# Group 0 of a fused attention and Fourier mixing kernel: plain products on resident weights, with the weights' combinations made for the later groups only

## The chip, the cores and the metric

One core of a Trainium2 chip. The metric is the device time of one execution in microseconds (us), the median of the executions named. Engines: PE is TensorE's matmuls, DVE VectorE, ACT ScalarE, POOL GpSimd, SP SyncE, which issues every large transfer of this kernel in one queue.

## The reference, cut to what matters

```python
# q, k, v: (8, 8, 576, 64) fp32; moe_w_ch1: (512, 2048), moe_w_ch2: (2048, 512)
x  = attention with softmax over the head dimension of q and over the sequence of k    # (8, 576, 512)
u  = x + real(fft(fft(x, axis=1), axis=2))
un = (u - mean) / sqrt(var + 1e-6)
return u + relu(un @ w_ch1) @ w_ch2
```

The kernel works in nine groups of 512 tokens. Each batch has a *front* (attention, Fourier transforms, normalisation); the front of batch g+1 is issued beside the two layers of group g.

## The kernel before

The two weight matrices arrive as 64-bit words that must be *converted* to fp32: 32 blocks of 128 x 512. From group 0 on both layers of the kernel before use Strassen's seven products of half blocks, so the weights are also *combined*: from four quarters, three more are made by adding and subtracting. Converted and combined weights are stored to scratch memory, from which every later group reloads them.

```python
def prepare(self, layer, p, places):
    w = self.wtile()                                        # one of 4 buffers
    for i in range(2):
        self.convert(places[i], w[:, 2 * i:2 * i + 2, :]...)        # ACT, DVE, POOL
    (self.b_side if layer else self.a_side)(lambda i: w[:, i, :], nc.gpsimd, nc.vector)
    if layer == 0:
        nc.sync.dma_start(self.w1s[p][:], w[:, 0:7, :])
        self.stream[p] = w                                  # used where it lies
    else:
        nc.sync.dma_start(self.w2s[:, :, p, :]..., w[:, 0:7, :])    # all 7 parts of pair p

def load(self, n):                                          # one reload: layer 2 takes ONE part of ALL 8 pairs
    ...
        self.nc.sync.dma_start(w[:], self.w2s[B_AT[ORDER[i - NP]]])

# group 0, in program order (start): products of layer 1 between the preparations
steps += [ready(0, 0), fetch_in(0, 3, 0)] + [ready(0, p) for p in range(1, 4)]
steps += jobs[0] + [ready(0, 4), ready(0, 5)] + jobs[1] + [ready(0, 6), ready(0, 7), fetch_in(1, 0, 12)]
steps += jobs[2] + [ready(1, 0), fetch_out(1, False), ready(1, 1)] + jobs[3]
for p in range(2, NP):
    steps += [fetch_out(p, p % 2 == 0), ready(1, p)]
return steps + [lambda i=i: blk.load(NP + i) for i in range(4)]
```

A tile framework orders the instructions of each engine and sets the semaphores; within an engine they run in that order.

Of the kernel before, what the change touches and what calls it, by code (L numbers as in the profile page):

```python
# [41 lines left out]
P = 128  # L43
# [13 lines left out]

A_AT = {1: 0, 2: 1, 3: 6, 4: 3, 5: 4, 6: 5, 7: 2}
B_AT = {1: 0, 2: 2, 3: 3, 4: 6, 5: 4, 6: 5, 7: 1}
ORDER = (1, 6, 5, 7, 2, 4, 3)  # L60
# [3 lines left out]

def merged(main, side):

    done = 0
    for i, step in enumerate(main):
        step()
        upto = (i + 1) * len(side) // len(main)  # L70
        while done < upto:
            side[done]()
            done += 1
    for step in side[done:]:
        step()
# [24 lines left out]
class _Block:  # L100
    def __init__(self, ctx, tc, q, kT, v, w1, w2, ft, cd, out):
# [27 lines left out]
        for t in (self.ZT, self.Zx, self.ZTr):  # L129
# [5 lines left out]
                      for p in range(2)]  # L135
        self.ft = c.tile([P, 7, NM], F32, name="ft")
# [27 lines left out]
    def wtile(self):  # L164
        return self.work.tile([P, NP, HD], F32, tag="w", name="w", bufs=4)

    def words(self, layer, f, place):

        if layer == 0:
            w1 = self.w1.bitcast(I32).rearrange("(k p) n -> p k n", p=P)  # L170
            self.nc.sync.dma_start(place.bitcast(I32).rearrange("p (k n) -> p k n", k=KT),
                                   w1[:, :, f * 2 * P:(f + 1) * 2 * P])
        else:
            w2 = self.w2.bitcast(I32).rearrange("(f p) n -> p f n", p=P)
            self.nc.sync.dma_start(place.bitcast(I32), w2[:, f, :])

    def convert(self, place, t):
        nc, V = self.nc, self.nc.vector
        pair = place.bitcast(I32).rearrange("p (n w) -> p n w", w=2)
        lo, hi = pair[:, :, 0], pair[:, :, 1]  # L180
        ti = t.bitcast(I32)

        nc.scalar.activation(lo, lo.bitcast(U32), ACT.Copy, scale=2.0 ** -29)

        V.tensor_scalar(out=ti, in0=hi, scalar1=3, scalar2=0x3FFFFFFF, op0=ALU.logical_shift_left,
                        op1=ALU.bitwise_and)
        V.scalar_tensor_tensor(out=ti, in0=hi, scalar=-(1 << 30), in1=ti, op0=ALU.bitwise_and, op1=ALU.bitwise_or)

        least = float(np.array(0x38100000, np.uint32).view(np.float32))
        nc.scalar.activation(hi.bitcast(F32), hi.bitcast(F32), ACT.Abs)  # L190
        V.scalar_tensor_tensor(out=t, in0=hi.bitcast(F32), scalar=least, in1=t, op0=ALU.is_ge, op1=ALU.mult)
        nc.gpsimd.tensor_tensor(out=ti, in0=ti, in1=lo, op=ALU.add)  # L192

    def a_side(self, at, e1, e2):

        e1.tensor_tensor(out=at(4), in0=at(2), in1=at(3), op=ALU.add)  # L196
        e1.tensor_tensor(out=at(2), in0=at(0), in1=at(2), op=ALU.subtract)
        e2.tensor_tensor(out=at(5), in0=at(4), in1=at(0), op=ALU.subtract)
        e2.tensor_tensor(out=at(6), in0=at(1), in1=at(5), op=ALU.subtract)

    def b_side(self, at, e1, e2):

        e1.tensor_tensor(out=at(4), in0=at(1), in1=at(0), op=ALU.subtract)
        e2.tensor_tensor(out=at(1), in0=at(3), in1=at(1), op=ALU.subtract)
        e1.tensor_tensor(out=at(5), in0=at(3), in1=at(4), op=ALU.subtract)
        e1.tensor_tensor(out=at(6), in0=at(2), in1=at(5), op=ALU.subtract)

    def prepare(self, layer, p, places):

        nc = self.nc  # L210
        w = self.wtile()
        for i in range(2):
            self.convert(places[i], w[:, 2 * i:2 * i + 2, :].rearrange("p a n -> p (a n)"))
        (self.b_side if layer else self.a_side)(lambda i: w[:, i, :], nc.gpsimd, nc.vector)
        if layer == 0:
            nc.sync.dma_start(self.w1s[p][:], w[:, 0:7, :])
            self.stream[p] = w
        else:
            nc.sync.dma_start(self.w2s[:, :, p, :].rearrange("s p n -> p s n"), w[:, 0:7, :])

    def load(self, n):

        g, i = divmod(n, NP + 7)
        if g > B:
            return
        w = self.wtile()
        if i < NP:
            self.nc.sync.dma_start(w[:, 0:7, :], self.w1s[i][:])
        else:
            self.nc.sync.dma_start(w[:], self.w2s[B_AT[ORDER[i - NP]]])  # L230
        self.stream[n] = w

# [227 lines left out]
    def norm(self, g):  # L460
# [31 lines left out]
        def all_stats():  # L492
# [4 lines left out]
        return unT, [all_stats] + pipelined(range(4), [normal, turn]) + [  # L497
            lambda: self.b_side(lambda i: unT[:, i], V, nc.gpsimd)]
# [7 lines left out]


# [35 lines left out]
    def up(self, g, unT, h):  # L543
# [3 lines left out]
        for j in range(NP // 2):  # L547
            pairs = (2 * j, 2 * j + 1)
            at = lambda i, j=j: h[:, 2 * j:2 * j + 2, i, :]

            def product(m, bank, first, last, pairs=pairs):
                def run(i):
                    w = self.stream[15 * g + pairs[i]]
                    for k in range(2):
                        nc.tensor.matmul(bank()[:, i, :], lhsT=w[:, A_AT[m], k * P:(k + 1) * P],  # L555
                                         rhs=unT[:, B_AT[m], k, :], start=first and i == 0 and k == 0,
                                         stop=k == 1,
                                         skip_group_check=True)
                return [lambda i=i: run(i) for i in range(2)]
# [4 lines left out]
            def other(i, at=at):  # L564
                def run(bank, u):
                    V.tensor_tensor(out=at(i), in0=bank[:], in1=u[:], op=ALU.add)  # L566
                    nc.scalar.activation(at(i), at(i), ACT.Relu)  # L567
                    if i == 2:
                        self.a_side(at, nc.gpsimd, nc.gpsimd)
                return run  # L570
# [5 lines left out]
    def used(self, n):  # L576
        self.stream.pop(n)
        if n >= NP:
            self.load(n + 4)

    def down(self, g, h):
        nc, V = self.nc, self.nc.vector

        def product(m, bank, first, last):
            n = 15 * g + NP + ORDER.index(m)

            def run(i, q):
                w = self.stream[n]
                for p in range(4 * q, 4 * q + 4):
                    nc.tensor.matmul(bank()[:, i, :], lhsT=h[:, p, A_AT[m], i * P:(i + 1) * P], rhs=w[:, p, :],  # L590
# [48 lines left out]
def kernel(ctx: ExitStack, tc: tile.TileContext, q, kT, v, w1, w2, ft,  # L639
# [34 lines left out]
    hpool = ctx.enter_context(tc.tile_pool(name="h", bufs=1))  # L674

# [3 lines left out]
    for step in front(0):  # L679
        step()  # L680
    for step in norm(0):
        step()
    for g in range(B + 1):
        unT = nexts.pop(g)
        h = hpool.tile([P, NP, 7, HD], F32, tag="h", name="h")
        jobs, down = blk.up(g, unT, h), blk.down(g, h)
        if g + 1 < B:
            side = front(g + 1)
        else:
            side = blk.reload() if g + 1 == B else []  # L690
        cut = len(side) * 2 // 3
        if g == 0:
            first = start(blk, jobs, h)
            merged(first, side[:cut])
        else:

            merged(flat(jobs), side[:cut])
        merged(down, side[cut:] + (norm(g + 1) if g < B else []))


def start(blk, jobs, h):


    at = h[:].rearrange("p a s n -> p (a s n)")
    inside = lambda r: at[:, r * 2 * D:(r + 1) * 2 * D]
    places = {}

    def fetch(layer, p, where):
        places[layer, p] = where
        for i in range(2):  # L710
            blk.words(layer, p + i * NP, where[i])

    def prepare(layer, p):
        blk.prepare(layer, p, places.pop((layer, p)))

    def fetch_in(layer, p, r):
        return lambda: fetch(layer, p, [inside(r), inside(r + 1)])

    def fetch_out(p, spare):
        def run():  # L720
            if spare:
                t = blk.work.tile([P, 7, 2, HD], F32, tag="unT", name="words", bufs=1)[:].rearrange(
                    "p a k n -> p (a k n)")
            else:
                t = blk.wtile()[:].rearrange("p a n -> p (a n)")
            fetch(1, p, [t[:, i * 2 * D:(i + 1) * 2 * D] for i in range(2)])
        return run

    def ready(layer, p):
        return lambda: prepare(layer, p)  # L730

    steps = [fetch_in(0, p, 2 * p) for p in range(3)] + [fetch_in(0, p, 2 * p - 2) for p in range(4, NP)]
    steps += [ready(0, 0), fetch_in(0, 3, 0)] + [ready(0, p) for p in range(1, 4)]
    steps += jobs[0] + [ready(0, 4), ready(0, 5)] + jobs[1] + [ready(0, 6), ready(0, 7), fetch_in(1, 0, 12)]
    steps += jobs[2] + [ready(1, 0), fetch_out(1, False), ready(1, 1)] + jobs[3]
    for p in range(2, NP):
        steps += [fetch_out(p, p % 2 == 0), ready(1, p)]
    return steps + [lambda i=i: blk.load(NP + i) for i in range(4)]
# [48 lines left out]
```

## Time and profile before

| | kernel before |
|---|---|
| time, median of 3 | 1392.67 us (1391.23 to 1393.92) |
| profiled span, mean granted clock of PE | 1384.5 us, 0.919 |
| group 0's first layer starts / its second layer / group 1 / group 2 | 110.25 / 289.8 / 338.2 / 464.5 us |

The prediction below shows the stages and the costliest waits. Two lines of the page give the whole: busy time of each engine, and PE's granted clock in 40 slices of 34.6 us, in tenths.

```profile
PE 1226.2 (89%) x5676; PEld 1003.1 (72%) x5676; DVE 580.0 (42%) x1146; ACT 326.7 (24%) x590; POOL 422.1 (30%) x350
...
PEclk7558785589999999999999999999999999999996
```

PE is busy 89% of the span, but the clock is 5 to 8 tenths in the first nine slices, that is up to 311 us. What releases PE between 110 and 290 us, in sum (us in all, times, longest):

```profile
engine line waited for: us in total, times, longest us
PE tr L486 <- DVE eo L479: 24.4, 2, 23.3
PE bb L555 <- DVE u L525: 23.9, 3, 8.7
```

And SP's queue late in that stretch. L219 stores one pair's combined quarters of W2, L230 reloads one part of all eight pairs:

```profile
257.44 0.38 SPq L219 DMA_DIRECT2D w2s<-w  x1
...
264.55 0.38 SPq L219 DMA_DIRECT2D w2s<-w  x1
...
275.77 0.38 SPq L219 DMA_DIRECT2D w2s<-w  x1
...
280.52 16.75 SPq L230 DMA_DIRECT2D w<-w2s  x5
```

The stores come as the preparations are done, here 7 to 11 us apart; the last is issued at 275.77, the reloads from 280.52 on, and only at 289.8 does the second layer start. Its first product needs a part from every pair, so by the code no product of the layer can start before the last pair is made, stored and reloaded. The trace alone doesn't show this wait: PE has no idle time just ahead of 289.8. After the 23.3 us of idle it turns batch 1's normalised tokens (from 260.3) and then works off the beginning of batch 2's front, which the framework put there.

### The profile page before, as it was taken

To read this page: it belongs to the slowest core of one execution; us is meant where nothing else is said; L and a number is where in the kernel's file an instruction comes from. 1 tells how busy PE (TensorE), PEld (TensorE's weight loads), DVE (VectorE), ACT (ScalarE), POOL (GpSimd) and SP (SyncE) were. 2 spreads that over 40 slices of the span, in tenths; PEclk is the share of its full clock that TensorE was granted. 3 is DMA by queue.
4 is the path that set the end of the run, shared out by engine and by line. 5 is a ranking of instruction groups with operands and counts; after the bars stand their busy time and mean duration, and the time that the engine had idled before them with its cause. 6 is when DMAs were issued, how large, how long until landed. Compare 5 with 4: busy or idle time off the path is not lost.

```text
span 1384.5 us, 14661 instructions
## 1 busy us (share of the span) xinstructions
PE 1226.2 (89%) x5676; PEld 1003.1 (72%) x5676; DVE 580.0 (42%) x1146; ACT 326.7 (24%) x590; POOL 422.1 (30%) x350
## 2 busy tenths in 40 slices
PE   4578677399899998999999999999999999999992
PEld 3437563288787876788778877887788778788882
DVE  3948876821513254335713542364234242502200
ACT  2624342410310142114301421142014101201200
POOL 1624566710530125003600450045013401321310
PEclk7558785589999999999999999999999999999996
DMA  5922334575342543156424542454253335455421
GB/s 170 306 68 69 137 128 163 190 265 164 141 152 88 172 159 146 67 167 198 158 98 138 193 159 77 145 197 152 88 146 130 150 103 174 150 178 179 165 102 45
DMA packets 90279, 203.46 MB, mean 147 GB/s; under 512 B 22241, under 2 KB 56033, under 8 KB 82145
## 3 DMA queue, kind: packets, MB, share of 16 engines
q1 hardware_dynamic: 90208, 202.52, 43.2%
q8 instruction: 45, 0.74, 0.2%
q14 instruction: 26, 0.20, 0.0%
HBM read 177.33 MB, written 29.88 MB: 150 GB/s over the span
## 4 chain that ended last, share of the span: by engine, by line
PE 74%; DVE 10%; POOL 6%; DMA 4%; issue 2%; ACT 1%; SPq 0%; POOLq 0%; DVEq 0%; ACTq 0%
PE bb L590 14%; PE bb L555 11%; PE bc L590 9%; PE ba L590 9%; PE ba L555 7%; PE bc L555 6%; PE acc L402 5%; DMA q<-in_q_dram 3%; PE acc L289 3%; PE acc L427 2%; POOL w L192 1%; PE acc L424 1%; PE tr L486 1%; PE acc L405 1%; POOL eo L384 1%
## 5 line engine op out<-in xcount | busy, mean ns | idle before, releaser
L555 PE MATMUL bb<-unT,w 128*128 128x256 f32 x864 | 218.8, 395 | 46.6 <-DVE u L525 39.6
L555 PEld LDWEIGHTS bb<-unT,w 128*128 128x128 f32 x864 | 166.5, 197 | 78.3 <-DVE u L525 46.3
L590 PE MATMUL bb<-w,h 128*128 128x256 f32 x864 | 198.5, 381 | 0.0
L590 PEld LDWEIGHTS bb<-w,h 128*128 128x128 f32 x864 | 161.5, 190 | 28.4 <-issue 7.3
L555 PE MATMUL ba<-unT,w 128*128 128x256 f32 x576 | 142.5, 387 | 0.0
L196 POOL TENSOR_TENSOR h<-h 128x512 f32<-128x512 f32 x36 | 46.1, 1279 | 313.4 <-ACT h L567 313.4
L555 PE MATMUL bc<-unT,w 128*128 128x256 f32 x576 | 140.5, 381 | 0.0
L590 PE MATMUL bc<-w,h 128*128 128x256 f32 x576 | 131.4, 381 | 0.0
L590 PE MATMUL ba<-w,h 128*128 128x256 f32 x576 | 128.0, 379 | 0.0
L590 PEld LDWEIGHTS bc<-w,h 128*128 128x128 f32 x576 | 107.5, 190 | 18.0 <-issue 4.4
L555 PEld LDWEIGHTS ba<-unT,w 128*128 128x128 f32 x576 | 109.2, 194 | 15.7 <-issue 1.0
L590 PEld LDWEIGHTS ba<-w,h 128*128 128x128 f32 x576 | 109.2, 190 | 15.4 <-issue 0.8
L555 PEld LDWEIGHTS bc<-unT,w 128*128 128x128 f32 x576 | 107.0, 190 | 15.3 <-DVE h L566 0.9
L567 ACT ACTIVATE h<-h 128x512 f32<-128x512 f32 x108 | 68.1, 631 | 190.8 <-DVE h L566 190.5
L604 POOL TENSOR_TENSOR x<-x,u 128x512 f32<-128x512 f32 x18 | 23.3, 1293 | 254.4 <-DVE u L528 172.2
L402 PE MATMUL acc<-ft,eo 128*128 128x289 f32 (+3 forms) x240 | 83.3, 472 | 7.5 <-POOL eo L386 7.4
L402 PEld LDWEIGHTS acc<-ft,eo 128*128 128x128 f32 (+3 forms) x240 | 39.6, 183 | 42.3 <-issue 26.0
L525 DVE TENSOR_TENSOR u<-bb,s 128x512 f32<-128x512 f32 x45 | 31.0, 689 | 89.1 <-PE bb L555 54.3
L318 POOL TENSOR_TENSOR q<-q,qm 128x512 f32<-128x512 f32 x36 | 41.8, 1170 | 82.2 <-DVE qm L317 33.1
L528 DVE TENSOR_TENSOR u<-bb,s 128x512 f32<-128x512 f32 x45 | 31.0, 689 | 77.5 <-PE bb L555 45.4
L289 PE MATMUL acc<-v,ks 128*128 128x128 f32 (+1 forms) x320 | 55.5, 317 | 6.1 <-ACT ks L277 4.1
L566 DVE TENSOR_TENSOR h<-bc,u 128x512 f32<-128x512 f32 x72 | 49.6, 689 | 24.0 <-PE bc L555 23.0
(134 smaller groups left out, 1540.0 us busy)
## 6 DMA issues: line engine op xcount, KB each, us to landing
w<-w2s SPq DMA_DIRECT2D x63, 1024.0 KB
w<-w1s SPq DMA_DIRECT2D x64, 896.0 KB
k<-in_kT_dram SPq DMA_DIRECT2D x32, 288.0 KB
h<-in_w_dram SPq DMA_DIRECT2D x18, 512.0 KB
v<-in_v_dram SPq DMA_DIRECT2D x32, 256.0 KB
q<-in_q_dram SPq DMA_DIRECT2D x32, 256.0 KB
w1s<-w SPq DMA_DIRECT2D x8, 896.0 KB
w2s<-w SPq DMA_DIRECT2D x8, 896.0 KB
```

Source lines behind the costliest of these rows:

```text
L196: e1.tensor_tensor(out=at(4), in0=at(2), in1=at(3), op=ALU.add)
L289: nc.tensor.matmul(pk, lhsT=ks[0:n, c, :], rhs=v[0:n, c, :], start=(c == 0), stop=(c == NC - 1))
L318: nc.gpsimd.tensor_tensor(out=heads, in0=heads, in1=spread(m), op=ALU.subtract)
L402: nc.tensor.matmul(pz, lhsT=eo[c][int(odds)][s, cols], rhs=self.ft[s, 3 * int(odds) + c, :], start=(c == 0), stop=(c == 2 and odds))
L427: nc.tensor.matmul(pb, lhsT=z(2 + k), rhs=self.cd[:, 2 + k, 0:HD - 1], start=(k == 0), stop=(k == 1))
L525: V.tensor_tensor(out=temp("u2"), in0=box["bb"][:], in1=box["s1"][:], op=ALU.add)
L528: V.tensor_tensor(out=temp("u3"), in0=box["bb"][:], in1=box["s1"][:], op=ALU.add)
L555: nc.tensor.matmul(bank()[:, i, :], lhsT=w[:, A_AT[m], k * P:(k + 1) * P], rhs=unT[:, B_AT[m], k, :], start=first and i == 0 and k == 0, s ...
L566: V.tensor_tensor(out=at(i), in0=bank[:], in1=u[:], op=ALU.add)
L567: nc.scalar.activation(at(i), at(i), ACT.Relu)
L590: nc.tensor.matmul(bank()[:, i, :], lhsT=h[:, p, A_AT[m], i * P:(i + 1) * P], rhs=w[:, p, :], start=first and i == 0 and p == 0, stop=p == ...
L604: nc.gpsimd.tensor_tensor(out=x, in0=x, in1=t[:], op=ALU.add)
```

## The change

The intent: group 0 alone computes whole products, two layers of 16 blocks on the converted weights where they lie in SBUF, so it needs no combined weights. The combinations, needed from group 1 on, are to be made beside its second layer. One large tile holds the converted W1, W2 and group 0's hidden layer; later it holds the ring of loads and the later hidden layers. The conversion is rewritten with one two-input DVE operation in place of two.

```diff
+        self.big = c.tile([P, 3 * NF * D], F32, name="big")
+        self.w1sb, self.w2sb, self.h0 = part(0), part(1), part(2)
...
+        def fetch(i):          # words of block i; most lie in w2sb until they are converted
+            if i < NF + 12 or i == NF + 13:
+                raw = self.w2sb[:, at:at + 2, :]...
+            else:              # W2's blocks 12, 14, 15: the place of the normalised input
+                    spare[0] = self.work.tile([P, 7, 2, HD], F32, tag="unT", name="words", bufs=1)
...
+            nc.scalar.activation(t, hi.bitcast(F32), ACT.Abs)
+            V.tensor_scalar_max(t, t, least)
-            V.tensor_scalar(out=ti, in0=hi, scalar1=3, scalar2=0x3FFFFFFF, ...)
+            V.tensor_scalar(out=ti, in0=ti, scalar1=3, scalar2=0x3FFFFFFF, ...)
             V.scalar_tensor_tensor(out=ti, in0=hi, scalar=-(1 << 30), in1=ti, ...)
-            V.scalar_tensor_tensor(out=t, in0=hi.bitcast(F32), scalar=least, in1=t, op0=ALU.is_ge, op1=ALU.mult)
+            nc.scalar.activation(lo, lo.bitcast(U32), ACT.Copy, scale=2.0 ** -29)
+            nc.gpsimd.tensor_tensor(out=out.bitcast(I32), in0=ti, in1=lo, op=ALU.add)
...
+    def combine(self, layer, p):
+        for i in range(2):     # three temporaries in turn, free when their store is done
+            tag = ("s1", "u2", "u3")[(2 * (NP * layer + p) + i) % 3]
+            t.append(self.work.tile([P, 2, HD], F32, tag=tag, name=tag, bufs=1))
...
+    def plain(self, g, unT):
+        def up(f):
+            n = ("ba", "bb")[f % 2]
+            ph = self.ps.tile([P, 512], F32, tag=n, name=n)
+            for k in range(KT):
+                nc.tensor.matmul(ph[:], lhsT=self.w1sb[:, f, k * P:(k + 1) * P], rhs=unT[...], ...)
+            if f % 2:
+                nc.vector.tensor_scalar_max(h[:, f, :], ph[:], 0.0)
+            else:
+                nc.scalar.activation(h[:, f, :], ph[:], ACT.Relu)
+        def part(i, n):        # 16 products of 512 columns into one bank, "bc"
...
+            for f in range(NF):
+                convert(f)
+                if f + 8 < 2 * NF:
+                    fetch(f + 8)
+                up[f]()
+            for f in range(NF):
+                if f == 0:
+                    fetch(NF + 12)
+                    fetch(NF + 14)
+                convert(NF + f)
+                after = {4: 8, 5: 9, 6: 10, 7: 11, 11: 13, 12: 15}
+                if f in after:
+                    fetch(NF + after[f])
+            combine = [lambda l=l, p=p: blk.combine(l, p) for l in range(2) for p in range(NP)]
+            combine[NP:NP] = [lambda i=i: blk.load(15 + i) for i in range(4)]
+            side += norm(1)
+            merged(down, mixed(side, combine))
```

Cut: the new numbering of the parts, the ring of loads in the large tile, and the old `start`, which goes.

## The prediction

> **What bounds the kernel now.** I read the windows view first, cut where the PE timeline shows stages to begin: group 0's first layer (110.25), its second layer (289.8), group 1 (338.2), group 2 (464.5).
>
> ```profile
> core 0: us, PE busy (x) PEld busy (x) DVE busy (x) ACT busy (x) POOL busy (x), PEclk, DMA share, GB/s
> ...
> 70.00:110.25 40.25, 28.44 (x62) 14.70 (x63) 22.32 (x59) 12.23 (x23) 9.91 (x11) 0.52 0.24 80
> 110.25:205.00 94.75, 70.89 (x345) 60.38 (x345) 78.07 (x128) 34.31 (x63) 52.63 (x43) 0.86 0.32 107
> 205.00:289.80 84.80, 51.61 (x155) 32.98 (x154) 58.30 (x111) 29.64 (x52) 50.00 (x42) 0.54 0.62 206
> 289.80:338.20 48.40, 48.40 (x226) 42.61 (x225) 9.26 (x19) 2.72 (x5) 5.90 (x5) 1.00 0.54 182
> 338.20:464.50 126.30, 121.09 (x569) 100.16 (x568) 40.33 (x79) 24.49 (x44) 34.23 (x28) 1.00 0.39 134
> 464.50:1384.50 920.00, 872.09 (x4185) 726.48 (x4184) 327.65 (x668) 194.39 (x352) 240.09 (x189) 0.98 0.42 142
> ```
>
> From 289.8 on PE is the bound: 1042 of 1095 us busy, granted clock 0.98 to 1.00. The 179.6 us from 110.25 to 289.8 are different: PE is busy 122 us, partly at half clock, and DVE is busy 136 us, POOL 103 us. Those are the weights' words being converted and combined. The PE timeline shows where it hurts (start, length, line):
>
> ```profile
> 133.15 1.89 PE L555 MATMUL ba<-unT,w 128*128 128x256 f32 x8
> 142.63 3.78 PE L555 MATMUL bb<-unT,w 128*128 128x256 f32 x8 [7.59 <-DVE u L525]
> ...
> 234.98 2.07 PE L427 MATMUL acc<-cd,Z 128*128 128x255 f32 x4
> 260.30 1.97 PE L486 MATMUL tr<-ident,eo 128*128 128x128 f32 x8 [23.26 <-DVE eo L479]
> ...
> 289.79 7.13 PE L590 MATMUL ba<-w,h 128*128 128x256 f32 x32
> 296.76 7.07 PE L590 MATMUL bb<-w,h 128*128 128x256 f32 x32
> ```
>
> PE waits 7.6 us for an eviction that stands behind conversions in DVE's queue, and 23.3 us for the next batch's normalisation, for the same reason. After such a gap eight instructions take 3.78 us in place of 1.89. The last two rows give the steady rate: 32 instructions in 6.9 us, 0.216 us each, two instructions to a product. The groups of 110 to 290 give what one conversion costs DVE:
>
> ```profile
> L191 DVE SCALAR_TENSOR_TENSOR w<-h,w 128x512 f32<-128x512 f32 x10 | 13.8, 1392 | 0.1
> L187 DVE SCALAR_TENSOR_TENSOR w<-h,w 128x512 int32<-128x512 int32 x10 | 10.4, 1051 | 0.0
> L185 DVE TENSOR_SCALAR w<-h 128x512 int32<-128x512 int32 x10 | 7.6, 774 | 0.2 <-PE bc L555 0.2
> L192 POOL TENSOR_TENSOR w<-w,h 128x512 int32<-128x512 int32 x10 | 14.2, 1423 | 5.3 <-DVE qrec L322 2.5 <-DVE w L191 2.0 <-issue 0.7
> ```
>
> The means are stretched: in the timeline the same L187 takes 0.69 us alone and up to 1.77 us beside POOL.
>
> **What the Trainium skill says.** "SBUF — State Buffer", section Who interferes with whom: GpSimd shares a read and write port pair with DVE; a DVE operation with two SBUF inputs, or a two-port mode, and a GpSimd operation lock each other out. The 0.69 against 1.77 us agrees. "TensorE: Matmul & The Clock Gate", section What's actually happening: half clock until about 3.4 us of sustained work, and again after an idle window. The trace agrees (3.78 after a gap of 7.6 us; a gap of 3.33 us at 362 did not bring it). "VectorE: DVE Perf Modes", section The perf-mode tier table: fp32 tensor_scalar in SBUF gets 2x, two-input operations 1x. The trace agrees: unstretched 0.42 us for L185, 0.69 for L187.
>
> **The change, part by part.** The instruction order of the two kernels can be compared, since the changed one builds; no time is taken from it. From group 2 on PE's order is the same. So I estimate when group 2 starts (464.5 now) and leave the 920 us after it.
>
> (a) Front of batch 0. Now group 0 starts at 110.25 with 8 of the 32 conversions done. In the new order all 16 of layer 1 stand before it, and two combinations. A conversion is now two tensor_scalar and one two-input operation: 0.42+0.42+0.69 = 1.53 us of DVE unstretched, against 0.42+0.69+0.69 = 1.80. Eight more are 12 us of DVE and 10 us of POOL (1.27 each). Between 70 and 110 DVE has 18 us idle and POOL 30, so most of it hides; a few operations stand on the chain of normalisation. Start: 112 us (110 to 119).
>
> (b) First layer. 16 x 4 products of 512 columns, two instructions of 2 x 0.216 each: 128 x 0.43 = 55 us, against 224 x 0.216 = 48 us for the seven products per pair. But of batch 1's front nearly nothing stands between them. What can stretch it is DVE: odd blocks are evicted there (relu), each bank has one buffer, and between the relu of block 1 and of block 15 DVE's order has 9 conversions, 23 combinations of 256 columns, 7 relus and batch 1's q work. Stretched: 9 x (0.75+0.75+0.91) = 21.7; 23 x 0.69 = 15.9; 7 x 0.69 = 4.8; q work 7.3; together 50 us, for 14 blocks that PE does in 14 x 3.45 = 48. In sum it balances, but it is loaded in front: 11.5 us lie between the relus of blocks 1 and 3, and 11.8 between 3 and 5, against 6.9 of PE. So I add 9 us of waiting and 3 us of half clock at the start. First layer: 67 us, ending at 179.
>
> (c) Second layer with the whole front of batch 1 beside it: 55 us of plain products, plus the front. From the timeline at full clock a front is: four k rows of 2.0, four q of 1.35, tails 2.0, first transform 10.1, second 5.0, turns 1.8, about 32 us. Three weight blocks wait for a buffer that frees only as layer 1 ends (two fetches of 512 KB, a conversion, a third fetch, a conversion: about 18 us); PE reaches them after 14 to 20 us, so little is lost. Four results share one bank: about 1 us each where nothing fills in. I put 8 us for these and for the normalisation chain. Total 95 us, group 1 starts at 274.
>
> (d) Group 1: 448 x 0.216 = 96.7, plus the front of batch 2, 32 us, plus the usual 2.5 us of waits: 131 us (now 126.3, because a third of that front was already done at 290). Group 2 starts at 405.
>
> So 464.5 - 405 = 59 us. PE's arithmetic grows by 14 us; the gaps that go are worth 73. The stores to the scratch weights and their reload are as many bytes as before and fall in a stage with room: at most some 15 MB in 67 us, 224 GB/s, against 302 GB/s reached at 35 to 70. I shade the gain to 57: 1392.7 - 57 = 1336 us.
>
> **Rivals.** *DVE and POOL remain the bound.* The conversions and combinations are all still there, now in 70 us in place of 180. If the port pair were wholly exclusive, POOL's work up to the end of layer 1 (about 63 us) and DVE's two-input and two-port work (about 70) would need 133 us from 33 on, so layer 1 could not end before 166, and at 85% use not before 189. For it: the stretched means. Against it: in 35 to 70 now, both did more unstretched work (about 42 us) than a wholly exclusive port allows in 35. It makes 10 to 20 us less gain: 1346 to 1356. *Head of line in the DMA queue.* All transfers are issued in order from one queue, stores that wait for combinations stand before fetches, and fetches of blocks 8 to 11 wait for conversions. Then ACT and DVE stand at a conversion while relus queue behind, and PE falls to half clock: 1350 to 1360. *PE alone is the bound.* Evictions keep up, layer 1 takes 58 and the second 90: 1322. *Nothing is won,* because what is removed returns as 14 us of products and a longer group 1: that needs 45 us of new waits, which I see no place for.
>
> **Range and chances.** The sum rests mostly on known PE counts; the uncertain terms are the start (+7), layer 1 (-9 to +15) and the second layer (-5 to +8). Range 1318 to 1356. The 2% line is at 1364.8, so faster 0.93, within 2% 0.06, slower 0.01.
>
> **What would show it.** Right: layer 1 starting at 110 to 119 and taking 60 to 75 us with DVE over 80% busy, PE's waits there being for DVE relus and none above 8 us; group 1 starting near 274; granted clock near 1.0 from 125 on, where it is 0.54 to 0.86 now; an unchanged 920 us after group 2's start. Wrong if PE waits for POOL or DMA in layer 1, if the blocks fetched last stop the second layer over 5 us, if batch 1's front leaves gaps over 10 us there, or if groups 2 to 8 get longer because loads and h share one tile.

## The result and the profile after

| | before | after |
|---|---|---|
| median, us (4 runs each, side by side) | 1391.95 (1387.39 to 1393.92) | 1329.29 (1327.89 to 1332.62) |
| profiled span, us | 1384.5 | 1327.7 |
| mean granted clock of PE | 0.919 | 0.968 |
| layer 1 starts / layer 2 / group 1 / group 2, us | 110.3 / 289.8 / 338.2 / 464.5 | 113.2 / 181.9 / 272.1 / 407.4 |

The ratio is 0.9558 with a 95% interval of 0.9528 to 0.9587: 4.4% less time. Ratios here and below are the mean time of one kernel's fast runs over that of the other's of the same rounds, so not quite the ratio of the medians. The result is correct.

The same two lines of the page:

```profile
PE 1216.9 (92%) x5484; PEld 951.8 (72%) x5484; DVE 556.6 (42%) x1145; ACT 317.5 (24%) x577; POOL 377.6 (28%) x314
...
PEclk9957899999999999999999999999999999999996
```

PE's busy time hardly moves, 1226 to 1217 us; an instruction at half clock counts with twice its length. What is gone is most of the idle time and half clock in the first nine slices; the end of batch 0's front, from 70 to 113 us, still has a clock of 0.53. The windows view of the changed kernel, cut at its own stages (busy us and count for each engine, PE's clock, share of the DMA engines, GB/s):

```profile
core 0: us, PE busy (x) PEld busy (x) DVE busy (x) ACT busy (x) POOL busy (x), PEclk, DMA share, GB/s
...
113.20:181.90 68.70, 59.57 (x130) 25.10 (x129) 51.30 (x84) 17.65 (x30) 34.54 (x33) 0.95 0.76 247
181.90:272.05 90.15, 87.80 (x322) 47.72 (x321) 38.15 (x99) 20.79 (x40) 15.37 (x14) 1.00 0.34 109
272.05:407.40 135.35, 131.10 (x647) 108.49 (x646) 61.26 (x134) 35.43 (x65) 41.04 (x33) 1.00 0.39 134
407.40:1327.70 920.30, 871.74 (x4185) 726.55 (x4183) 329.05 (x668) 194.32 (x352) 239.94 (x189) 0.98 0.41 142
```

From 110 to 464.5 us the kernel before needed 354.3 us; the same work, from layer 1 to group 2, now takes 407.4 - 113.2 = 294.2. The 920 us that follow are as long as before. In the second layer PE is busy 87.8 of 90.2 us at full clock: batch 1's front has matmuls beside it. In the kernel before, its transforms, its normalisation and the beginning of batch 2's front stood alone at 205 to 290 us, at clock 0.54 with PE idle 33 us.

The PE timeline of the changed kernel (start, length, line; in brackets the idle time ahead and its releaser):

```profile
113.23 3.60 PE L568 MATMUL ba<-unT,big 128*128 128x512 f32 x8
...
136.53 5.40 PE L568 MATMUL bb<-unT,big 128*128 128x512 f32 x8 [4.54 <-DVE big L571]
...
156.10 5.37 PE L568 MATMUL bb<-unT,big 128*128 128x512 f32 x8 [2.37 <-DVE big L571]
...
178.47 3.60 PE L568 MATMUL bb<-unT,big 128*128 128x512 f32 x8
181.91 7.03 PE L580 MATMUL bc<-big 128*128 128x512 f32 x16
...
191.97 0.48 PE L337 MATMUL acc<-v,ks 64*128 64x128 f32 x2 [2.04 <-DVE ks L328]
...
272.05 1.89 PE L638 MATMUL ba<-unT,big 128*128 128x256 f32 x8
```

A block is eight instructions and takes 3.60 us at full clock. Its result lies in one of two PSUM banks, ba and bb, until a relu has taken it out (L571 on DVE for odd blocks). After the gap of 4.54 us one took 5.40, after 2.37 us one took 5.37: half clock. The waits of both layers together:

```profile
engine line waited for: us in total, times, longest us
PE bb L568 <- DVE big L571: 9.1, 4, 4.5
PE acc L337 <- DVE ks L328: 2.0, 1, 2.0
```

At the end of layer 1, DVE and then SP's queue:

```profile
175.04 0.43 DVE L235 TENSOR_TENSOR u<-big,u 128x256 f32<-128x256 f32 x1 [4.30 <-DMA w2s<-u]
...
188.35 0.43 DVE L212 TENSOR_SCALAR big<-big 128x512 f32<-128x512 f32 x1 [5.55 <-ACT big L211]
...
190.34 1.38 DVE L214 TENSOR_SCALAR big<-big 128x512 int32<-128x512 int32 x1
191.64 0.27 DVE L328 COPY ks<-tr 64x128 f32<-64x128 f32 x1
```

```profile
171.76 4.55 SPq L261 DMA_DIRECT2D w2s<-u  x2
...
182.10 9.70 SPq L197 DMA_DIRECT2D words<-in_w_dram  x3
```

L235 and L233 combine W2 and wait for earlier stores out of the three temporaries. L197 fetches the last three blocks of words into the place of layer 1's input; it can start only as layer 1 ends, at 182.1, and its third fetch is issued at 191.5. The conversion L212 follows at 188.35, and k's copy (L328, which takes turned columns of k out of PSUM for PE's next products) at 191.64, in order behind it. PE loses only 2.0 us by it.

### The profile page after: what moved, and what is told of

It is laid out like the page before. It is cut to its first block, busy times and chain, and to the rows that moved or that the text cites. A ratio compares the mean times of both kernels' runs of the same rounds, so it can differ in the third digit from the quotient of the medians.

```text
span 1327.7 us, 14389 instructions
## 1 busy us (share of the span) xinstructions
PE 1216.9 (92%) x5484; PEld 951.8 (72%) x5484; DVE 556.6 (42%) x1145; ACT 317.5 (24%) x577; POOL 377.6 (28%) x314
## 4 chain that ended last, share of the span: by engine, by line
PE 76%; DVE 9%; POOL 3%; issue 3%; DMA 2%; ACT 1%; SPq 0%; POOLq 0%; DVEq 0%
PE bb L673 13%; PE bb L638 10%; PE bc L673 8%; PE ba L673 8%; PE ba L638 6%; PE bc L638 6%; PE acc L450 5%; PE bc L580 3%; PE acc L337 3%; DMA q<-in_q_dram 2%; PE acc L475 2%; PE acc L472 1%; PE bb L568 1%; PE tr L534 1%; PE tr L324 1%
## 5 line engine op out<-in xcount | busy, mean ns | idle before, releaser
L638 PE MATMUL bb<-unT,big 128*128 128x256 f32 x768 | 190.5, 388 | 21.8 <-DVE u L608 15.6
L638 PEld LDWEIGHTS bb<-unT,big 128*128 128x128 f32 x768 | 145.1, 193 | 49.2 <-DVE u L608 19.4
L673 PE MATMUL bb<-big 128*128 128x256 f32 x768 | 177.3, 382 | 0.0
L673 PEld LDWEIGHTS bb<-big 128*128 128x128 f32 x768 | 143.3, 190 | 26.0 <-issue 7.3
L638 PE MATMUL bc<-unT,big 128*128 128x256 f32 x512 | 126.3, 383 | 0.0
L638 PE MATMUL ba<-unT,big 128*128 128x256 f32 x512 | 125.5, 384 | 0.0
L673 PE MATMUL bc<-big 128*128 128x256 f32 x512 | 117.3, 381 | 0.0
L673 PE MATMUL ba<-big 128*128 128x256 f32 x512 | 113.8, 379 | 0.0
L673 PEld LDWEIGHTS bc<-big 128*128 128x128 f32 x512 | 95.3, 190 | 16.4 <-issue 4.4
L673 PEld LDWEIGHTS ba<-big 128*128 128x128 f32 x512 | 97.0, 190 | 13.8 <-issue 0.8
L638 PEld LDWEIGHTS ba<-unT,big 128*128 128x128 f32 x512 | 95.8, 191 | 13.3 <-issue 0.6
```

The costliest lines, as they stand in the source:

```text
L638: nc.tensor.matmul(bank()[:, i, :], lhsT=w[:, WA_AT[m], k * P:(k + 1) * P], rhs=unT[:, B_AT[m], k, :], start=first and i == 0 and k == 0, ...
L673: nc.tensor.matmul(bank()[:, i, :], lhsT=h[p][:, A_AT[m], i * P:(i + 1) * P], rhs=w[:, p, :], start=first and i == 0 and p == 0, stop=p == ...
```

## The experiments

Each kernel was timed in three rounds beside the kernel before. "After" is 1329.29 us in the first measurement and 1330.40 when it was repeated. Where stages are given, they are of one profiled execution. Layer 1 starts between 108.9 and 113.2 us in the profiles of the changed kernel and of 3, 4, 7 and 8, which are the same up to there, so read the lengths of stages and not their starts. 1 to 8 ran on one chip, 9 to 11 on a second and 12 on a third; the kernel before took 1389.18, 1388.22 and 1386.92 us beside them.

**1. The new conversion alone.** The kernel before with the new conversion.

```diff
-        V.scalar_tensor_tensor(out=t, in0=hi.bitcast(F32), scalar=least, in1=t, op0=ALU.is_ge, op1=ALU.mult)
+        nc.scalar.activation(t, hi.bitcast(F32), ACT.Abs)
+        V.tensor_scalar_max(t, t, least)
```

> The kernel before with the changed kernel's conversion alone (two tensor_scalar and one two-input DVE operation, in place of one and two; the absolute value first). Theory (the gain is PE's waits behind the whole DVE queue, most of which stays here): DVE's work per conversion falls from 1.80 to 1.53 us unstretched and one hand-over between ACT and DVE goes, so 8 to 15 us less, 1377 to 1384 us. Rival (the cheaper conversion is the gain): under 1355.

Measured: 1390.49 us (1389.37 to 1392.61), ratio 1.0016 (0.9986 to 1.0046). No gain; I had expected one. PE's waits from 105 to 300 us of this kernel:

```profile
engine line waited for: us in total, times, longest us
PE tr L484 <- DVE eo L477: 25.4, 3, 13.9
PE bb L553 <- DVE u L523: 22.6, 3, 8.1
PE tr L484 <- ACT unT L488: 12.2, 1, 12.2
```

They stand at the same two places as before (normalisation, and the eviction of layer 1). 11.3 us of the first row lie ahead of layer 1; without them the sum is 49 us, no smaller than the 48 of the kernel before, and 12.2 us of it are now for ACT. So the cheaper arithmetic is no part of the gain by itself.

**2. The kernel before without conversions.** The three engines' operations are replaced by one copy; the result is wrong.

```diff
-        (the two activations, the three DVE operations and the POOL operation of convert)
+        nc.scalar.activation(t, hi.bitcast(F32), ACT.Copy)
```

> The kernel before with the conversion's arithmetic taken away (one ACT copy remains of two ACT, three DVE and one POOL operation; wrong result on purpose), all transfers and combinations kept. Theory (conversions in DVE's queue make the gaps of group 0): the stage of 179.6 us falls to some 100 to 110, so 1310 to 1328 us. Rival (the gaps come of the transfers, the four ring places or the buffers): at least 1350.

Measured: 1348.06 us (1344.75 to 1351.50), ratio 0.9717 (0.9680 to 0.9754): 40 us less, where I had expected 61 to 79 (the rival said at least 1350, and is missed by 2 us). A third to a half of what was to go stays. From the start of layer 1 to that of the second layer (236.35):

```profile
core 0: us, PE busy (x) PEld busy (x) DVE busy (x) ACT busy (x) POOL busy (x), PEclk, DMA share, GB/s
99.00:155.00 56.00, 51.81 (x271) 44.75 (x270) 35.54 (x73) 23.89 (x46) 27.05 (x24) 0.97 0.44 145
155.00:236.35 81.35, 53.02 (x187) 34.02 (x185) 41.69 (x84) 26.71 (x48) 39.92 (x39) 0.70 0.62 210
```

137 us in place of 180. Up to 155 us PE runs at clock 0.97. But then it is busy only 53 of 81 us at clock 0.70: layer 1's last products end at 176, and from there the rest of batch 1's front and the beginning of batch 2's run with no layer to fill in, until every pair of W2 has been combined, stored and reloaded. Here the second layer's first product waits for its reload:

```profile
236.35 9.87 PE L581 MATMUL ba<-w,h 128*128 128x256 f32 x32 [1.42 <-DMA w<-w2s]
```

The order costs time even where conversion costs nothing.

**3. All relus on ACT**, in the changed kernel.

```diff
-            if f % 2:
-                nc.vector.tensor_scalar_max(h[:, f, :], ph[:], 0.0)
-            else:
-                nc.scalar.activation(h[:, f, :], ph[:], ACT.Relu)
+            nc.scalar.activation(h[:, f, :], ph[:], ACT.Relu)
```

> The changed kernel with all 16 relus of group 0's first layer on ACT, none on DVE. Theory (PE's 9.1 us of waits there, and the 3.6 us of half clock after them, come of relus that stand behind conversions in DVE's queue): the waits for DVE go; ACT has 51 of 69 us free, but its own queue holds operations that wait for transfers, so some of it comes back: 1318 to 1326 us. Rival (DVE and POOL together bound the layer through their shared port): no gain, 1327 to 1333.

Measured: 1334.12 us (1332.02 to 1336.40), ratio 0.9609 (0.9579 to 0.9639): no gain. Layer 1 took 69.3 us. PE no longer waits for DVE's relus; it waits for ACT's (6.9 us in three waits), 2.6 us for what the profile gives as a combination on POOL, and 3.8 us for k's copy in the second layer.

**4. Three banks in turn in layer 1**, in the changed kernel.

```diff
-            n = ("ba", "bb")[f % 2]
+            n = ("ba", "bb", "bc")[f % 3]
```

> The changed kernel with three PSUM banks in turn in group 0's first layer in place of two, all else the same. Theory: a relu has two blocks' time (6.9 us) in place of one before PE needs its bank, so waits fall from 9.1 to under 2 us and the half clock goes: 1316 to 1322 us. Rival (port bound): PE waits at the end of the layer in place of its middle, 1326 to 1332.

Measured: 1334.46 us (1329.06 to 1337.64), ratio 0.9607 (0.9571 to 0.9643): no gain. Layer 1 took 65.5 us, 3 less, but the second 97.4, 7 more. The PE timeline at its start:

```profile
191.21 0.79 PE L337 MATMUL acc<-v,ks 64*128 64x128 f32 x2 [7.50 <-DVE ks L328]
```

The second layer starts 6 us earlier (3 of them because layer 1 does in this profile), and after its first sixteen instructions PE stands 7.5 us for k's copy, which ends at 191 as it does in the changed kernel. The wait has moved.

**5. W1's combinations held back** until the relu of block 7, in the changed kernel (a one-column write into each temporary that depends on that relu; overwritten later).

```diff
+        if layer == 0:
+            for a in t:
+                nc.scalar.copy(a[:, :, 0:1], self.h0[:, 7, 0:2].unsqueeze(2))
```

> The changed kernel with layer 1's weight combinations held back until the relu of block 7 (a small ACT copy of that relu's output is written to their places first; right result). The order of the changed kernel has them among the conversions, not beside the second layer as its words say. Theory A (weights' chain): DVE, POOL and the transfer queue are freer for the second matrix's fetches and conversions, PE's waits in layer 1 fall to 3 to 6 us: 1320 to 1327. Theory C (the last fetches wait for layer 1's buffer anyway, and combinations then crowd the second layer): 1327 to 1335.

Measured: 1335.48 us (1327.71 to 1339.52), ratio 0.9611 (0.9569 to 0.9654): no gain. Layer 1 took 72.2 us with 10.8 us of waits, no fewer than in the changed kernel; the longest is 5.5.

**6. The changed kernel without conversions** (wrong), as in 2.

```diff
-            (the same six operations of convert)
+            nc.scalar.activation(out, hi.bitcast(F32), ACT.Copy)
```

> The changed kernel with the conversion's arithmetic taken away as in the run on the kernel before (one ACT copy remains; wrong result on purpose). Theory A, after two runs that moved PE's waits without a gain (the weights' chain, conversions to combinations to stores to the last fetches, ends the stage and not PE's own queueing): from layer 1 to group 1 it falls from 159 us to 142 to 148, PE's own work, and the front gains 3 to 8 us: 1306 to 1318. Theory B (PE's products and the front of batch 1 already bound it): 1322 to 1330. Beside the 40 us that the same cut took off the kernel before, it tells how much of the old stage was conversions and how much the round trip through the scratch weights.

Measured: 1303.75 us (1301.17 to 1305.14), ratio 0.9385 (0.9351 to 0.9420): 27 us less than the changed kernel, more than I expected. The windows of its layer 1 and second layer:

```profile
core 0: us, PE busy (x) PEld busy (x) DVE busy (x) ACT busy (x) POOL busy (x), PEclk, DMA share, GB/s
101.36:158.96 57.60, 57.49 (x129) 25.14 (x129) 24.90 (x57) 11.84 (x20) 15.17 (x19) 0.96 0.87 297
158.96:248.90 89.94, 88.54 (x325) 48.04 (x324) 35.75 (x93) 21.34 (x40) 14.45 (x14) 1.00 0.37 117
```

Layer 1 starts 11.8 us earlier (101.4 for 113.2; by the scatter of this start, 8 to 12) and takes 11.1 us less (57.6 for 68.7); PE is busy in all of it. The second layer is as long as before, 89.9 for 90.2. From layer 1 to group 1 it is 147.5 us, inside theory A's 142 to 148. With 2 this gives a square:

| median, us | with conversions | without | conversions cost |
|---|---|---|---|
| kernel before | 1388.68 | 1348.06 | 41 |
| kernel after (repeated) | 1330.40 | 1303.75 | 27 |
| the arrangement saves | 58 | 44 | |

So 44 us of the 58 are the arrangement without any conversion, and the remaining 14 are conversions that it hides better.

**7. 14 of 16 blocks in both layers** (wrong), in the changed kernel.

```diff
-            for f in range(4 * n, 4 * n + 4):
+            for f in range(4 * n, min(4 * n + 4, 14)):
```

(and the last two blocks of the first layer left out.)

> The changed kernel with 14 of 16 blocks in both layers of group 0, the size of the seven-product form's work (wrong result on purpose). If PE bounds group 0: 12 to 14 us less, 1315 to 1318. If the weights' chain bounds layer 1 and PE only the second layer: 6 to 9 us less, 1320 to 1324. If neither: under 3 us.

Measured: 1325.98 us over four runs: one of 1337.68, three 1317.36, 1318.03 and 1333.92, so the time decides little. The profiled run, 1317.36, owes 4.3 us to an earlier start of layer 1 (108.9). In the profiled run 13.8 us of PE's work (32 instructions of 0.43) are gone; layer 1 takes 6.7 us less, the second layer none, since PE then waits 4.6 us for k's copy. From layer 1 to group 1 it is 153.1 us in place of 158.9 (5.8 less, for 13.8 us of work). What PE itself does is thus not all of the bound in the second layer's first third.

**8. The changed kernel again**, unaltered, on the chip of 5 to 7.

> The changed kernel unaltered, as the yardstick for the runs beside it: 1327 to 1333 us, ratio 0.953 to 0.960. Group 1 starts 158 to 160 us after layer 1 of group 0, whenever that starts.

Measured: 1330.40 us (1327.06 to 1334.35), ratio 0.9574 (0.9539 to 0.9609). From layer 1 to group 1: 159.1 us, first time 158.9. Single executions of this same kernel differ by up to 7 us.

**9. The last words fetched early**, into rows 10 to 15 of the hidden layer, whose blocks of layer 1 then follow the conversions.

```diff
-                    spare[0] = self.work.tile([P, 7, 2, HD], F32, tag="unT", name="words", bufs=1)
+                at = {12: 10, 14: 12, 15: 14}[f]
+                raw = self.h0[:, at:at + 2, :].rearrange("p a n -> p (a n)")
...
+                if f == 2:
+                    for i in (12, 14, 15):
+                        fetch(NF + i)
+                if f < 10:
+                    up[f]()
```

> The changed kernel, but the last three blocks of W2's words are fetched into rows of the hidden layer that layer 1 has not written yet (10 to 15), instead of into the normalised input's place, which frees only as layer 1 ends; the blocks of layer 1 that write these rows come after the conversions in program order. Theory (in layer 1 and behind it the waits are one chain: conversions, temporaries freed by stores, the one transfer queue, the last fetches; only removing a link helps): the fetch of the words moves from 182 us to before 165, k's copy no longer stands behind conversions that end at 191 us, and the second layer's waits of 2.4 us and some of the layer's 9 us go; length from the start of layer 1 to group 1 about 152 us in place of 159, time 1318 to 1328. Rival (TensorE's own work and the combinations set the stage, late fetches cost nothing, as the prediction said): 1328 to 1336, no gain.

Measured: 1337.35 us (1335.22 to 1340.02), ratio 0.9629 (0.9609 to 0.9648): slower than the changed kernel, against both my theory and, by a little, the rival. The fetch did move ahead. But see DVE's timeline:

```profile
196.69 0.43 DVE L233 TENSOR_TENSOR u<-big,u 128x256 f32<-128x256 f32 x1 [4.03 <-DMA w2s<-u]
...
197.82 0.28 DVE L326 COPY ks<-tr 64x128 f32<-64x128 f32 x1
```

k's copy now ends at 198, no longer behind a conversion but behind combinations of W2, and those wait for the stores out of the three temporaries (4.0 us in the first row here, 5.1 us for an earlier one). Layer 1 took 76 us: all conversions now lie in it. From layer 1 to group 1 it is 168.6 us, where I expected 152.

**10. The same with three banks.**

```diff
-            n = ("ba", "bb")[f % 2]
+            n = ("ba", "bb", "bc")[f % 3]
```

> The same with three result banks in turn in layer 1. By the theory the third bank, which gained nothing alone because the wait moved to k's copy behind the last conversions, should now gain, as that place is free: 3 to 6 us below the kernel with the early fetch alone, 1313 to 1324, length from layer 1 to group 1 about 148 us. Rival: again no gain from the bank, within 2 us of the kernel with the early fetch.

Measured: 1337.36 us (1335.96 to 1338.20), ratio 0.9633 (0.9619 to 0.9647): the rival's case, no gain from the bank. Layer 1 is 5 us shorter than in 9 and k's copy, at 198 again, takes it back in a wait of 7.95 us. From layer 1 to group 1 it is 168.4 us, where the theory said 148.

**11. The second layer made to wait for the last combination**, in the changed kernel. Two copies of one column out of W2's last temporaries into the hidden layer do it (one token's hidden values are wrong; the result stayed within the tolerance).

```diff
-            merged(down, mixed(side, combine))
+            for step in combine:
+                step()
+            for f, t in enumerate(blk.made[-2:]):
+                nc.scalar.copy(blk.h0[:, f, 2 * P:2 * P + 1], t[:, 1, 0:1])
+            merged(down, side)
```

> The changed kernel with its second layer of group 0 made to wait for the last combination of W2 (two copies of one column out of the last temporaries into the hidden layer, so the result is wrong on purpose), and the combinations ahead of it in program order. It still needs no reload from scratch memory. Theory (the gain of the arrangement is that the second layer no longer waits for the weights' preparation, and that batch 1's front has matmuls beside it): the last combination ends about 205 us at the earliest, so the second layer starts 20 to 25 us later and part of the front runs alone at half clock: 1345 to 1360. Rival (only the round trip through scratch memory mattered, or waiting work is filled with the front): 1330 to 1338.

Measured: 1349.10 us (1347.03 to 1357.13), ratio 0.9729 (0.9696 to 0.9763): 19 us more than the changed kernel, as the theory said, and outside the rival's range. Between the end of layer 1 and the second layer, and in the second layer:

```profile
core 0: us, PE busy (x) PEld busy (x) DVE busy (x) ACT busy (x) POOL busy (x), PEclk, DMA share, GB/s
...
184.90:211.79 26.89, 14.50 (x71) 11.40 (x70) 22.19 (x55) 10.15 (x20) 8.97 (x9) 0.68 0.68 228
211.79:291.48 79.69, 79.38 (x257) 40.17 (x256) 28.81 (x71) 14.70 (x30) 11.65 (x10) 1.00 0.15 46
```

For 26.9 us PE has only the front, is busy 14.5 us at clock 0.68, and in the second layer 10 us of the 90 are saved because part of the front is done. The loss is 26.9 - 10.5 = 16.4 us in these two stages and 2.5 in layer 1 (71.2 for 68.7), which is the 19 of the time. The edit also sets the combinations ahead of batch 1's front in program order; how much of the 19 us that gives by itself was not measured.

**12. Three links at once**: three banks, the last words fetched early into places that are free anyway (batch 1's two x tiles and the unused part of layer 1's input tile, so that layer 1's order stays), seven temporaries in place of three.

```diff
+                if f == 15:
+                    raw = self.un0[:, 4:6].rearrange("p a k n -> p (a k n)")
+                else:
+                    self.xpart(1, 0, int(f == 14))
+                    raw = self.xs[1, int(f == 14)][:].rearrange("p a n -> p (a n)")
...
+                if f == 8:
+                    for i in (12, 14, 15):
+                        fetch(NF + i)
...
+            n = (2 * (NP * layer + p) + i) % 7
+            if n < 3:
+                (as before)
+            else:
+                t.append(self.halves()[:, 0:D].rearrange("p (a n) -> p a n", n=HD))
```

> The changed kernel with three links of the preparation chain taken away at once, the arithmetic kept: three result banks in turn in layer 1; the last three blocks of W2's words fetched early into places that are free anyway (the next batch's two x tiles and the unused part of the normalised input's tile), so the order of layer 1 is not touched; seven temporaries in place of three for the combinations, so they wait less for their stores. Theory of a chain of waits (each link alone gave nothing because the next took its place): now it must gain, from the start of layer 1 to group 1 about 149 to 154 us in place of 159, time 1320 to 1326, and k's first copy ends before 188 us (191 in the changed kernel, 198 with the early fetch alone). Rival (what is left in this stage is the conversions' and combinations' own work in the queues of VectorE and GpSimd, not their waits): 158 to 166 us, 1329 to 1338, and k's copy again at 190 us or later, with VectorE busy above 80% of layer 1.

Measured: 1330.38 us (1329.40 to 1332.83), ratio 0.9587 (0.9571 to 0.9603): the same time as the changed kernel. DVE's timeline at the end of layer 1, and the windows of layer 1, second layer and group 1:

```profile
187.40 0.28 DVE L333 COPY ks<-tr 64x128 f32<-64x128 f32 x1 [6.29 <-PE tr L332]
```

```profile
core 0: us, PE busy (x) PEld busy (x) DVE busy (x) ACT busy (x) POOL busy (x), PEclk, DMA share, GB/s
112.06:180.20 68.14, 58.83 (x129) 24.71 (x129) 52.60 (x85) 20.04 (x35) 36.48 (x32) 0.96 0.69 241
180.20:268.20 88.00, 87.54 (x317) 47.18 (x316) 41.59 (x108) 19.11 (x37) 15.41 (x15) 1.00 0.28 89
268.20:406.75 138.55, 133.68 (x649) 109.91 (x648) 59.54 (x128) 33.67 (x62) 39.10 (x33) 0.99 0.41 143
```

The waits at this place are gone as the theory said: DVE has been idle for 6.3 us when k's copy comes at 187.40, released by PE, and the second layer takes 88.0 us. But layer 1 takes 68.1 us as ever (2.4 us of it are its first block at half clock, 6.03 us for 3.60, which the changed kernel did not have; PE waits five times 0.4 to 1.9 us for relus, and once 3.1 us for what the profile gives as a conversion on POOL), and group 1 takes 138.6 us in place of 135.3, since part of PE's work lies there now (133.7 us busy for 131.1). From layer 1 to group 1 it is 156.2 us, between the theory's 149 to 154 and the rival's 158 to 166, and from layer 1 to group 2 294.7 us, for 294.2. So the theory was right on where the waits were and wrong on their worth. The rival's number for VectorE (above 80% of layer 1) failed as well: 52.6 of 68.1 us is 77%.

None of the kernels with a correct result is faster than the changed one beyond its scatter.

## Why the prediction was right

**The sum.** Predicted 1336 us in 1318 to 1356; measured 1329.29. Group 2 starts 57.1 us earlier (464.5 - 407.4), where 59 were predicted before shading and 57 after; the profiled spans differ by 56.8. The medians differ by more, 62.7 us, because the profiled execution of before was a fast one of its kind (1386.24 us, below all four of the side-by-side runs), and the stages were read from it while the gain was taken off the median. That is where 6 of the 7 us between prediction and result lie. Part of the closeness is luck: stage (c) is 4.8 us shorter and stage (d) 4.3 us longer than predicted, and the two cancel.

**(a) Start of layer 1**: predicted 112, measured 113.2, and 108.9 to 113.2 over five profiles of kernels that are the same up to there. Right; conversions put 8 to 12 us there by experiment 6.

**(b) Layer 1**: predicted 67 us, measured 68.7. The terms hold: 55 us of PE (experiment 6, with nothing to wait for, took 57.6, its first block at half clock), 9 us of waits (measured 9.1) and 3 us of half clock (5.40 and 5.37 for 3.60, so 3.6). The place of the half clock was wrong: the first blocks ran at full speed, and it came after gaps in the middle, so the clock was 0.95 and not near 1.0 from 125 us on (in 9, 10 and 12 the first block did take 4.64 to 6.03 us). The busy share of DVE was put too high, over 80%; it was 51.3 of 68.7 us, 75%. What loads DVE there in front is right, and so is that no wait passes 8 us: the longest was 4.54. As to the cause of these waits, experiments 3, 4, 5 and 12 eased them each in another way and none shortened the whole; experiment 6, which removes the conversions' work, did by 11 us in this layer. What still has to be shown is whether it is the engines' sum of work or their blocking of each other that gives the 11 us; no run here separates the two.

**(c) Second layer and batch 1's front**: predicted 95 us, measured 90.2. The term that was mis-sized is the 8 us for the bank and the normalisation chain: 2.0 us for k's copy and 0.3 for the bank were lost. The statement that the late fetches cost little held: 2.0 us. Experiments 9 and 10 fetched them early and gained nothing; experiment 12 took that wait away and the time stayed.

**(d) Group 1**: predicted 131 us, measured 135.3. PE's work was 131.1 us where I had 128.7, and the waits 4.2 us in place of 2.5.

**The tail**: 920 us unchanged was predicted, 920.3 measured.

**Readings that were off.** The prediction puts DVE's 136 and POOL's 103 us of 110 to 290 down to conversions and combinations. By the groups of the trace 75 of DVE's are (63 and 12) and 65 of POOL's (37 and 28); the rest belongs to the fronts and to layer 1's results. Its table of the perf modes has a row for tensor_tensor and none for the scalar_tensor_tensor of L187; that L187 takes as long as a tensor_tensor of its size is shown by the trace (0.69 us, and 0.69 for L385). The range, 1318 to 1356, is not the sum of its three terms, which would be 1322 to 1366.

**The reason.** The prediction said that the stages end on DVE's preparation of weights, and that group 0's gaps go because preparation no longer stands between PE's instructions. The runs make this narrower. The gain is not the cheaper conversion (1: nothing), and mostly not the hiding of conversions (14 of 58 us by the square). It is the arrangement, 44 us of 58 even without conversions: the second layer of group 0 no longer stands behind weights that have to be combined, stored and reloaded, and batch 1's front therefore runs beside matmuls. Of this, experiment 11 shows 19 us, as the cost of the wait for the combinations alone (with the change of order that it brings). A kernel that has this wait but no reload from scratch memory is still 39 us faster than before. How these 39 split between the reload, the resident W1 and the better hiding was not measured, so that part of the cause is argued and not shown.

**The rivals.** DVE and POOL as the full bound (1346 to 1356) fell with the time, though in part it lives: the conversions still cost 27 us. The queue's head of line (1350 to 1360) fell; the queue does hold a load of k back, to 191.89, behind the third fetch of words, but no wait of PE comes of it: the 2.0 us are for k's copy on DVE, which stands behind conversions of those words. PE alone (1322) is not reached, since layer 1 has its waits. Nothing won fell.

## What to carry to other kernels

Ask of every stage what its *first* instruction needs: a layer whose first product needs a part of every block of a matrix cannot overlap with that matrix's preparation, however short the preparation's operations are made. It can pay to do more arithmetic once (14 us of PE here) if that arithmetic runs on data as it comes, and the next batch's front then fills in beside it at full clock. When one wait has been eased and the time stays, follow the next stage before easing another: a third bank here shortened the first layer by 3 to 5 us, twice, and both times gave it back within 20 us at the same copy; with three reliefs at once the loss reappeared one group later.

## What the Trainium skill lacked or had wrong

- "TensorE: Matmul & The Clock Gate", section What's actually happening, has half clock return after an idle window of about 3.4 us in a free-running count. Here shorter gaps, as the profile gives them, were enough: 2.37 us in the changed kernel (the block after it took 5.37 us in place of 3.60) and 2.36 us in experiment 7 (5.37 again). A gap of 2.21 us in experiment 9 was not (3.70 us), nor one of 3.49 us in experiment 10 (3.67 us). What else counts was not found out.
- The same page, section Architectural detail, says that VectorE's and ScalarE's queues are strictly first in, first out. This agrees: in the changed kernel the transpose that k's copy reads ended at 189.0 us and the copy at 191.9; in experiment 9 at 194.5 and 198.1, behind whatever stood ahead of it. The page does not draw the consequence that removing a wait ahead of such a queue only helps if the next entry is ready; experiments 4 and 10 show it (7.5 and 7.95 us of PE's waiting stood at that copy).
- "SBUF — State Buffer", section Who interferes with whom, gives the lock between VectorE and GpSimd, and the stretched lengths agree (L214 0.43 us and 1.38 us, in the fence of the changed kernel). It gives no way to tell what the lock costs a stage with a mix of operations: DVE was busy 51.3 us and POOL 34.5 us of a layer of 68.7 us, so neither their sum nor either alone is the length.
- No page used here tells how a transfer that waits for its producer or its place holds later ones in the one queue that issues them all: in the changed kernel the second store of L261 was issued at 175.95, 3.5 us after the record of the first ends, and the third fetch of L197 at 191.47, 8.6 us after that of the second; batch 1's next load of k came only behind it, at 191.89.
